# A decay-attention and soft-MoE kernel on one core: late weight loads, an early slot turn, and a second layer by column halves

## The chip, the core and the metric

The kernel runs on one core of one Trainium2 chip, as one launch. The metric is the device time in microseconds. Before the change the median of three runs is 163.58 us (163.57 to 164.32). Everything below was read from one profiled execution of that kernel, whose own time is 163.59 us.

## The reference

The work is two layers. The first is causal attention with a decay per head, done in blocks; its output, laid out as 3072 tokens of 512, is the input of a soft mixture of 8 experts with 4 slots each.

```python
# q, k, v: (4, 8, 768, 64); lam: (8,); per block of 64 tokens:
intra = einsum('bhic,bhjc->bhij', qb, kb) * Dmask        # lam ** (i - j), i >= j
out   = einsum('bhij,bhjd->bhid', intra, vb) + einsum('bhid,bhde->bhie', qb * lam_pow, state)
state = lam ** 64 * state + einsum('bhsd,bhse->bhde', kb * rev_pow, vb)

# x: (3072, 512), phi: (512, 32), w1: (8, 512, 1024), w2: (8, 1024, 512)
logits = x @ phi
d = softmax(logits, axis=0);  slot_input = (d.T @ x).reshape(8, 4, 512)
for e in range(8):
    slot_out[e] = relu(slot_input[e] @ w1[e]) @ w2[e]
out = softmax(logits, axis=1) @ slot_out
```

All data are float32. w1 and w2 are 16.8 MB each, q, k and v 6.3 MB each, and the output is 6.3 MB.

## The kernel before

**Attention.** The kernel takes chunks of 128 tokens for all heads, two sequences at a time, which it calls a pair; there are 12 pairs (NP), with p counting them. A pass over pair p runs `carried(p)` (the state's share, which reads q), `values(p)` (reads v), a copy of the result to XT by ScalarE, and `state(p)` (the state's update, which reads v and the turned keys kd). Then it starts the next pair with `scores(p + 1)`, whose products land in the PSUM banks w0 to w3 and are multiplied by the mask into `at` by four VectorE instructions, while GpSimd scales q. `turn_k` turns the keys of pair p + 1 where a state still has to be made; the last chunk of a sequence (pairs 5 and 11) needs none. Beside that, every second pass turns the exponentials e of the token softmax on TensorE (`turn_e`) and multiplies them with the tokens into slot sums (`slots`), in bank w2, from which `at` must have been read first.

**Loads.** All transfers are issued by one queue, SyncE's (SP), strictly in the order in which the code asks for them. Two homes each for q, k and v are filled two pairs ahead. w1 (32 loads of 512 KB, "early") goes into 27 slab homes and 8 others, w2 (32 loads of 512 KB, "late") into whatever is free at the end: 3 spare slabs, the homes of q, k, v, kd, mask, at, xt and x, and slabs whose w1 has been used. From p = 10 on, `next_load` puts a late load where it would have loaded q, k or v, and holds it behind a TensorE instruction of that pass (`behind`).

**The mixture.** `first(Q, ...)` multiplies the slot inputs with w1 for experts 4Q to 4Q + 3, and the result, after ReLU, is turned into hz[Q] by two VectorE instructions. The second layer multiplies hz with w2 in quads: four matmuls, one per expert, each 32 rows of the array, into four partition groups of one bank. `blocks` says in which order. FS = (4, 0) says that the first four blocks of Q = 0 come whole, 512 columns wide, and that all others are stored by column halves of 256. `second(0)` computes everything whole and the first column half's rest into bank r, and `second(1)` the rest of the second half into bank w0. The slot outputs are copied to `so`, spread over the partitions (`spread`, giving s4), and `put` makes one output tile: two matmuls, a copy by ScalarE or VectorE in turn, a transfer of 256 KB to y. There are 24 puts, 12 for each column half. PUTS and LAST say where they stand: 9 of the first half within `second(1)`, the other 15 behind it. The pair t = 0 is computed in full float32 from CR and so, with four matmul records where the others have two.

The helper class `InOrder` records all operations, so every row of the profile names line L49; the tiles tell them apart.

Of the kernel before, what the change touches and what calls it, by code (L numbers as in the profile page):

```python
# [11 lines left out]
ALU = mybir.AluOpType  # L12
# [4 lines left out]
NB = S // P  # L17
T = B * NB
HP = H // 2
D = H * DH  # L20
SL = 32
# [4 lines left out]
NP = T // 2  # L26
NSLAB = 27
NWARM = 9
FS = (4, 0)
HD = D // 2  # L30
SPARE = 3

PUTS = ((2, (0,)), (6, (9,)))
LAST = (2, 0, 1)

SENT = ((1, 1, 1, 1), (1, 1, 1, 1), (1, 0, 1, 1))
# [18 lines left out]
def decay_attn_soft_moe(  # L55
# [13 lines left out]
    pe, dve, act, pool, sp = (InOrder(tc, x) for x in (nc.tensor, nc.vector, nc.scalar, nc.gpsimd, nc.sync))  # L69
# [3 lines left out]
    loads = ctx.enter_context(tc.tile_pool(name="loads", bufs=2))  # L73
    work = ctx.enter_context(tc.tile_pool(name="work", bufs=1))
# [5 lines left out]
    def bank(tag):  # L80
        return ps.tile([P, 512], F32, tag=tag, name=tag)


    PAIR = [(b, n) for b in range(0, B, 2) for n in range(NB)]
# [19 lines left out]

    wt = {}
    early = [(Q, kc, q) for Q in range(2) for kc in range(4) for q in range(4)]
    blocks = [[], []]
    for Q in range(2):
        mid = (8 + FS[Q]) // 2
        blocks[0] += [(Q, f) for f in range(mid)]  # L110
        blocks[1] += [(Q, f) for f in range(mid, 8)]
    late = [(Q, f, i) for part in blocks for Q, f in part for i in range(2)]
    early.reverse()
    late.reverse()
# [12 lines left out]
    def load_late(pool_=None, tag="slab", bufs=None):  # L127
        Q, f, i = late.pop()
        kw = {} if bufs is None else {"bufs": bufs}
        t_ = (pool_ or slabs).tile([P, 2, 512], F32, tag=tag, name="w2t", **kw)  # L130
        go = sp.dma_start(out=t_, in_=w2[4 * Q + 2 * i:4 * Q + 2 * i + 2, f].rearrange("e p d -> p e d"))
        for y in range(2):
            wt["w2", Q, 2 * i + y, f] = t_[:, y, :]
        return go
# [9 lines left out]
    for a in range(2):  # L144
        for hh in range(2):
            sp.dma_start(
                out=phi_sb[64 * a:64 * a + 64, 2 * hh:2 * hh + 2],
                in_=phi[64 * hh:64 * hh + 64].rearrange("c (g a) s -> a c g s", a=2)[a],
# [17 lines left out]
    mask = work.tile([P, 2, HP, P], F32, tag="mask", name="mask")  # L166
    for hh in range(2):
        for hp in range(HP):
            y = hh * HP + hp
            dve.tensor_tensor_scan(  # L170
                out=mask[:, hh, hp, :],
# [34 lines left out]
    wb = [bank("w0"), bank("w1"), bank("w2"), bank("w3")]  # L206
# [6 lines left out]
    def behind(ins, earlier):  # L213
        how = mybir.DependencyInfo(mybir.DependencyClass.Sync, mybir.DependencyReason.DATA)
        tc.add_manual_dep(ins.ins, earlier.ins.name, how, reason="kept behind")
        return ins
# [27 lines left out]
    def turn_k(p, x, tk):  # L244
        for hp in range(HP):
            c = slice(hp * P, hp * P + P)
            pe.transpose(tk[:, c], IN["k", p][:, x, c], ident)
        dve.tensor_tensor(
            out=kd[:, x],
            in0=tk.rearrange("p (a b c) -> p a b c", a=HP, b=2),  # L250
            in1=kpow.broadcast_to([P, HP, 2, DH]),
            op=ALU.mult,
        )
# [17 lines left out]
    def carried(p):  # L271
        qs = IN["q", p].rearrange("p x (a i) -> p x a i", a=HP)
        first = None
        for x in range(2):
            for hp in range(HP):
                for hh in range(2):
                    mm = pe.matmul(
                        out=place(x, hh, hp),
                        lhsT=st[rows(hh), x, hp],
                        rhs=qs[rows(hh), x, hp],  # L280
                        start=(x == 0 and hp < 2),
                        stop=True,
                        skip_group_check=True,
                    )
                    first = first or mm
        return first
# [90 lines left out]
    def turn_e():  # L377
        dp = rb[:, P:2 * P]
        pe.transpose(dp, e, ident)
        act.copy(out=d, in_=dp)  # L380
# [24 lines left out]
    def next_load(p, which, at_):  # L405

        if p + 2 < NP:
            behind(load_in(p + 2, which), at_)
        else:
            behind(load_late(loads, which, 2), at_)  # L410

    def next_weights(p, point, at_):
        for _ in range(SENT[p % 3][point]):
            if early:
                behind(load_early(1), at_)
            elif run["spare"] < SPARE:
                run["spare"] += 1
                behind(load_late(bufs=NSLAB), at_)
# [7 lines left out]
    for p in range(NP):  # L426
        b, n = PAIR[p]
        even = p % 2 == 0
        more = p + 1 < NP
        g = (p - 2) // 2 if p >= 2 else None  # L430


        m1 = carried(p) if n > 0 else None
        if g is not None and even:
            new = highest(g)
            weigh(g, new)


        m2 = values(p)
        next_load(p, "k", m1 or m2)  # L440
        if p == NP - 1:
            load_late(work, "mask")
        next_weights(p, 0, m2)
        XT[p] = keep.tile([P, 2, HP, P], F32, tag="xt", name="xt", bufs=2)
        for hh in range(2):
            copy = act.copy if more or hh == 0 else dve.tensor_copy
            copy(
                out=XT[p][:, :, 2 * hh:2 * hh + 2],
                in_=xb[hh].rearrange("p (x a i) -> p x a i", x=2, a=2),
            )  # L450
        if g is not None and not even:
            gather(g)
        if n < NB - 1:
            m2 = state(p)
        next_load(p, "q", m2)
        next_weights(p, 1, m2)
        if p == NP - 2:
            load_late(work, "kd")
        if not more:
            break  # L460


        m3, m4 = scores(p + 1)
        if PAIR[p + 1][1] > 0:
            scale_q(p + 1)
        next_load(p, "v", m3)
        next_weights(p, 2, m4)


        turns = [lambda x=x: turn_k(p + 1, x, wb[x]) for x in range(2)] if PAIR[p + 1][1] < NB - 1 else []  # L470
        if g is not None and even:
            turn_e()
        m5 = m4
        if even:
            for f in turns:
                f()
        else:
            for x in range(2):
                m5 = turn_x(p - 1, x)
                for f in turns[x:x + 1]:  # L480
                    f()
            for x in range(2):
                turn_x(p, x)
        next_weights(p, 3, m5)


        if not even:
            logits((p - 1) // 2)
        elif g is not None:
            slots(g)  # L490
        if p == 0:
            reduce_selectors()
# [10 lines left out]
    g = G - 1  # L503
# [30 lines left out]
    for n, (w_, x_) in enumerate(terms):  # L534
        for kc in range(4):
            pe.matmul(
                out=si[SL * kc:SL * kc + SL, 0:P],
                lhsT=w_,
                rhs=x_.rearrange("p (h g a c) -> p g a h c", h=2, g=2, a=2)[:, kc // 2, kc % 2],
                start=(n == 0),  # L540
                stop=True,
# [118 lines left out]
    stack(three)  # L660
    assert not late

    po = bank("r")

    def quad(dst, Q, f, w, start, stop):
        for q in range(4):
            pe.matmul(
                out=dst[SL * q:SL * q + SL],
                lhsT=hz[Q][:, 4 * f + q],
                rhs=w(q),  # L670
                start=start,
                stop=stop,
                skip_group_check=True,
            )

    def second(part, dst, fill):
        todo = []
        for Q, x in blocks[part]:
            if x < FS[Q]:
                todo.append((dst, Q, x, lambda q, Q=Q, x=x: wt["w2", Q, q, x]))  # L680
            else:
                half = (8 - FS[Q]) // 2
                for i in range(2):
                    f = FS[Q] + 2 * ((x - FS[Q]) % half) + i
                    todo.append((
                        dst[:, 0:HD], Q, f,
                        lambda q, Q=Q, x=x, i=i: wt["w2", Q, q, x][:, i * HD:(i + 1) * HD],
                    ))
        for n, (d_, Q, f, w) in enumerate(todo):
            if n in fill:  # L690
                fill[n]()
            quad(d_, Q, f, w, n == 0, n == len(todo) - 1)

    so = work.tile([P, D], F32, tag="qpow", name="so")
    po1 = bank("w0")
    obanks = ("a0", "a1", "s", "w1", "w3", "r")
    nput = [0]
    s4 = []
# [27 lines left out]
        sp.dma_start(out=dst.rearrange("(a p) c -> p a c", p=P), in_=o)  # L726
        nput[0] += 1

    pairs = [(t, half) for half in range(2) for t in range(0, T, 2)]
    pairs.reverse()  # L730

    def give(n):
# [1 line left out]
            t, half = pairs.pop()  # L734
            put(t, half)

    second(0, po, {})
    act.copy(out=so[:, 0:HD], in_=po[:, 0:HD])
    dve.tensor_copy(out=so[:, HD:D], in_=po[:, HD:D])

    def split():
        s4.append(spread(len(s4)))
# [1 line left out]
    fill = {}  # L744
    for n, x in PUTS:
        fill[n] = lambda x=x: [split() if y == 0 else give(y) for y in x]
    second(1, po1, fill)
    dve.tensor_tensor(out=so[:, HD:D], in0=so[:, HD:D], in1=po1[:, 0:HD], op=ALU.add)
    for y in LAST:
        split() if y == 0 else give(y)  # L750
    give(len(pairs))
# [57 lines left out]
```

## Time and profile before

| What | Value |
|---|---|
| median of three runs | 163.58 us (163.57 to 164.32) |
| the profiled execution | 163.59 us |
| its span | 161.8 us |
| TensorE busy (matmul records) | 144.8 us, 89%, 2304 records |
| TensorE weight loads | 112.6 us, 2304 records |
| VectorE, ScalarE, GpSimd busy | 92.9, 50.9, 35.6 us |
| HBM read, written | 52.50 MB, 6.29 MB |

The profiled execution is 1.79 us longer than its span, which runs from the program's first instruction to its last. Matmul times of single records overlap, so a stretch is better read from when its records start. A float32 matmul leaves two records. The DMA share in a row by stretches is over 1 where all 16 engines work all the time: about 1.05 with loads, 1.09 with stores.

### The profile page before, as it was taken

The numbers are of one execution on the slowest core, as the hardware profiler recorded it, in microseconds if no ns is written. First come the engines' busy times: TensorE is split into PE (matmuls) and PEld (weight loads), VectorE is DVE, ScalarE is ACT, GpSimd is POOL, SyncE is SP. The second block draws the span as 40 slices with busy tenths as digits, with TensorE's granted clock in tenths as the row PEclk, the third lists the DMA queues.
The fourth block names the chain that finished last, engine by engine and source line by source line (L and its number), as shares of the span: only waits on it lengthen the run. The fifth ranks groups of instructions, "written<-read, shape, count | busy, mean of one in ns | idle before, by whom it ended". The sixth has DMA issues, their size and how long they took to land.

```text
span 161.8 us, 5407 instructions
## 1 busy us (share of the span) xinstructions
PE 144.8 (89%) x2304; PEld 112.6 (70%) x2304; DVE 92.9 (57%) x203; ACT 50.9 (31%) x118; POOL 35.6 (22%) x52
## 2 busy tenths in 40 slices
PE   6999899999997999999999899798999999999000
PEld 6988898979894989699878889476332355768000
DVE  4599581767638273938193854455589971458300
ACT  3020234202540254025402162033237951328100
POOL 1006060423206000505060511400038810000000
PEclk9999999999999999999999999999999999999855
DMA  4999999999999999999999957899999999499993
GB/s 113 358 388 410 412 413 408 409 414 409 411 418 408 412 408 415 409 413 412 409 417 397 402 222 225 300 272 359 402 407 408 402 407 406 189 313 352 383 383 127
DMA packets 30408, 59.14 MB, mean 366 GB/s; under 512 B 2736, under 2 KB 8880, under 8 KB 30384
## 3 DMA queue, kind: packets, MB, share of 16 engines
q1 hardware_dynamic: 30384, 58.80, 96.0%
q8 instruction: 18, 0.29, 0.7%
q14 instruction: 6, 0.05, 0.1%
HBM read 52.50 MB, written 6.29 MB: 363 GB/s over the span
## 4 chain that ended last, share of the span: by engine, by line
PE 68%; DMA 15%; DVE 5%; SPq 2%; issue 2%; DVEq 0%; ACT 0%; ACTq 0%
PE a L49 28%; PE w L49 25%; DMA q<-qT 10%; PE r L49 10%; DMA v<-vN 5%; PE s L49 4%; SPq L49 2%; DVE at L49 2%; DVE o L49 2%; DVE st L49 1%; DVEq L805 0%; ACT s L49 0%; DVE e L49 0%; ACTq L49 0%; DVEq L49 0%
## 5 line engine op out<-in xcount | busy, mean ns | idle before, releaser
L49 POOL TENSOR_TENSOR q<-q,qpow 128x512 f32<-128x512 f32 x20 | 25.1, 1278 | 74.9 <-PE w L49 74.9
L49 DVE TENSOR_TENSOR at<-w,mask 128x512 f32<-128x512 f32 x48 | 29.8, 684 | 6.9 <-PE w L49 6.9
L49 PE MATMUL w<-q,k 64*128 64x128 f32 x384 | 25.2, 280 | 1.1 <-DMA q<-qT 1.1
L49 PEld LDWEIGHTS w<-q,k 64*128 64x128 f32 x384 | 22.8, 189 | 2.4 <-issue 1.0
L49 ACT COPY xt<-a 128x512 f32<-128x512 f32 x23 | 12.4, 589 | 36.3 <-PE a L49 36.3
L49 PE MATMUL a<-at,v 128*64 128x128 f32 x384 | 23.6, 276 | 0.0
L49 PEld LDWEIGHTS a<-at,v 128*64 128x64 f32 x384 | 20.7, 137 | 2.1 <-issue 2.1
L49 DVE SCALAR_TENSOR_TENSOR st<-st,qpow,s 128x128 f32<-128x128 f32 x32 | 9.0, 345 | 20.2 <-PE s L49 20.2
L49 ACT COPY x<-a 128x512 f32<-128x512 f32 x22 | 12.3, 588 | 17.8 <-PE a L49 17.8
L49 PE MATMUL a<-ident,xt 128*128 128x128 f32 x96 | 13.8, 278 | 0.0
L49 PEld LDWEIGHTS a<-q,st 64*64 64x64 f32 x320 | 8.6, 132 | 5.5 <-POOL q L49 4.5
L49 DVE TENSOR_TENSOR kd<-w,mask 128x512 f32<-128x512 f32 x18 | 11.6, 683 | 0.0
L49 PE MATMUL a<-q,st 64*64 64x128 f32 x320 | 11.3, 276 | 0.1
L49 PEld LDWEIGHTS a<-ident,xt 128*128 128x128 f32 x96 | 10.6, 140 | 1.1 <-issue 0.2
L49 PE MATMUL s<-v,kd 128*64 128x64 f32 x320 | 11.1, 222 | 0.0
L49 PEld LDWEIGHTS s<-v,kd 128*64 128x64 f32 x320 | 10.6, 138 | 0.2 <-DVE kd L49 0.2
L49 PE MATMUL w<-ident,k 128*128 128x128 f32 x72 | 10.3, 274 | 0.0
L49 PE MATMUL r<-w2t,hz 128*32 128x256 f32 (+1 forms) x128 | 8.8, 432 | 0.0
L49 PEld LDWEIGHTS w<-ident,k 128*128 128x128 f32 x72 | 8.2, 141 | 0.3
L49 PE MATMUL w<-x,e 128*32 128x512 f32 (+1 forms) x72 | 6.4, 456 | 1.9 <-DVE at L49 1.8
L49 PE MATMUL a<-w1t,e 128*32 128x512 f32 x64 | 7.1, 594 | 0.5 <-DVE e L49 0.5
L49 ACT CAST ct<-part 32x256 fp32r<-32x256 f32 x18 | 7.2, 402 | 1.1 <-DVE part L49 0.9
(112 smaller groups left out, 152.6 us busy)
## 6 DMA issues: line engine op xcount, KB each, us to landing
w1t<-w_x SPq DMA_DIRECT2D x32, 512.0 KB, 9.5
w2t<-w_x SPq DMA_DIRECT2D x32, 512.0 KB, 9.4
v<-vN SPq DMA_DIRECT2D x12, 512.0 KB, 9.1
y<-o SPq DMA_DIRECT2D x24, 256.0 KB, 4.5
k<-kT SPq DMA_DIRECT2D x11, 512.0 KB, 8.7
q<-qT SPq DMA_DIRECT2D x11, 512.0 KB, 8.5
k<-kT SPq DMA_DIRECT2D x2, 256.0 KB, 3.1
q<-qT SPq DMA_DIRECT2D x2, 256.0 KB, 3.5
```

What stands on the lines that cost most here:

```text
L49: return self._tc.keep_in_program_order(f(*args, **kwargs))
```

## The change

- FS becomes (0, 0): all of w2 is stored and multiplied by column halves. `blocks` lists the eight blocks of the first half for both Q, then the eight of the second. `second(half)` computes one half into one bank (r, then w0) and copies it to its half of `so`; the add of two parts goes.
- In PUTS the 9 puts within the second half stand after 4 quads and no longer after 6. The full-precision pair t = 0 becomes the last put of each half and no longer the first.
- Late loads of the last two passes are no longer held behind a chosen matmul: each is asked for where its home's last reader has been written, and waits for that reader alone. The order becomes k, q, v, kd, k, mask, q.
- Where no keys turn (p = 4 and p = 10), `turn_e` stands ahead of `scores(p + 1)`.

```diff
-FS = (4, 0)
+FS = (0, 0)
-PUTS = ((2, (0,)), (6, (9,)))
+PUTS = ((2, (0,)), (4, (9,)))
...
+    blocks = [[(Q, x) for Q in range(2) for x in range(4 * half, 4 * half + 4)] for half in range(2)]
...
         if p + 2 < NP:
             behind(load_in(p + 2, which), at_)
-        else:
-            behind(load_late(loads, which, 2), at_)
...
+        if p == NP - 2:
+            load_late(loads, "k", 2)
         m1 = carried(p) if n > 0 else None
+        if p >= NP - 2:
+            load_late(loads, "q", 2)
...
-        if p == NP - 1:
-            load_late(work, "mask")
...
         if p == NP - 2:
+            load_late(loads, "v", 2)
             load_late(work, "kd")
...
+        if g is not None and even and not turns:
+            turn_e()
         m3, m4 = scores(p + 1)
...
+        if p == NP - 2:
+            load_late(loads, "k", 2)
+            load_late(work, "mask")
...
-        if g is not None and even:
+        if g is not None and even and turns:
             turn_e()
...
+    po = [bank("r"), bank("w0")]
+    def second(half, fill):
+        todo = [(Q, x, i) for Q, x in blocks[half] for i in range(2)]
+        for n, (Q, x, i) in enumerate(todo):
             if n in fill:
                 fill[n]()
+            for q in range(4):
+                pe.matmul(
+                    out=po[half][SL * q:SL * q + SL, 0:HD],
+                    lhsT=hz[Q][:, 4 * (2 * (x % 4) + i) + q],
+                    rhs=wt["w2", Q, q, x][:, i * HD:(i + 1) * HD],
...
+        copy = act.copy if half == 0 else dve.tensor_copy
+        copy(out=so[:, half * HD:(half + 1) * HD], in_=po[half][:, 0:HD])
...
-    pairs = [(t, half) for half in range(2) for t in range(0, T, 2)]
+    pairs = [(t, half) for half in range(2) for t in (*range(2, T, 2), 0)]
...
-    second(1, po1, fill)
-    dve.tensor_tensor(out=so[:, HD:D], in0=so[:, HD:D], in1=po1[:, 0:HD], op=ALU.add)
+    second(1, fill)
```

TensorE's order from the second layer's start to the end of the second half. Before: (w2t are weights, r, w_1829 and the a_ and s names are banks, ct and CR the softmax weights, s_1906 the spread slot outputs, so their source)

```order
L49 MATMUL r<-w2t,hz 32x512 x16
L49 MATMUL r<-w2t,hz 32x256 x48
L49 MATMUL w_1829<-w2t,hz 32x256 x8
L49 MATMUL w_1904<-so,blk 128x256
L49 MATMUL w_1829<-w2t,hz 32x256 x16
L49 MATMUL a_1925<-so,CR 128x256 x2
L49 MATMUL a_1931<-s_1906,ct 128x256 x2
```

TensorE's order in the same place after the change:

```order
L49 MATMUL r<-w2t,hz 32x256 x64
L49 MATMUL w_1828<-w2t,hz 32x256 x8
L49 MATMUL w_1903<-so,blk 128x256
L49 MATMUL w_1828<-w2t,hz 32x256 x8
L49 MATMUL a_1916<-s_1905,ct 128x256 x2
```

The 16 wide matmuls became 32 narrow ones, 16 of them in the second half; 8 matmuls and no longer 16 stand between the spread and the first put, and CR is no longer in the first put. Behind the nine puts 48 matmuls of the second half are left, where there were 24.

TensorE's order around `scores(11)` in the pass p = 10. Before: (e are the exponentials, x the tokens, the w_ names the banks of the scores)

```order
L49 MATMUL w_147<-q,k 128x128
L49 MATMUL w_146<-q,k 128x128
L49 MATMUL w_147<-q,k 128x128
L49 MATMUL r<-ident,e 128x128
L49 MATMUL w_146<-x,e 32x512 x4
L49 MATMUL a_142<-q,st 64x128
```

TensorE's order at the start of the same scores after the change:

```order
L49 MATMUL a_143<-at,v 64x128 x4
L49 MATMUL s<-v,kd 64x64 x16
L49 MATMUL r<-ident,e 128x128
L49 MATMUL w_144<-q,k 128x128
L49 MATMUL w_145<-q,k 128x128
```

The one turn of e went ahead of the 16 matmuls of the scores; the slot sums (w_146<-x,e) stay behind them.

SP's late loads from p = 10 on, numbers kept since a lower number is asked for earlier. Before, for the homes k, q, kd, v, k, mask, q:

```order
L49 DMA w2t_1415<-w2_x 128x2x512 [waits DMAHW6_49,PE_49]
L49 DMA w2t_1440<-w2_x 128x2x512 [waits DMAHW7_49,PE_49,Pool_49]
L49 DMA w2t_1442<-w2_x 128x2x512 [waits DMAHW0_49,DVE_49,PE_49]
L49 DMA w2t_1466<-w2_x 128x2x512 [waits DMAHW1_49,PE_49]
L49 DMA w2t_1506<-w2_x 128x2x512 [waits DMAHW3_49,DMAHW2_49,PE_49]
L49 DMA w2t_1508<-w2_x 128x2x512 [waits DVE_49]
L49 DMA w2t_1514<-w2_x 128x2x512 [waits DMAHW4_49,PE_49,Pool_49]
```

SP's same seven loads after the change, for the homes k, q, v, kd, k, mask, q:

```order
L49 DMA w2t_1373<-w2_x 128x2x512 [waits DMAHW6_49,PE_49]
L49 DMA w2t_1391<-w2_x 128x2x512 [waits DMAHW7_49,PE_49,Pool_49]
L49 DMA w2t_1442<-w2_x 128x2x512 [waits DMAHW0_49,PE_49]
L49 DMA w2t_1444<-w2_x 128x2x512 [waits DMAHW1_49,DVE_49]
L49 DMA w2t_1470<-w2_x 128x2x512 [waits DMAHW3_49,DMAHW2_49,PE_49]
L49 DMA w2t_1472<-w2_x 128x2x512 [waits DVE_49]
L49 DMA w2t_1494<-w2_x 128x2x512 [waits DMAHW4_49,PE_49,Pool_49]
```

The loads keep their count and nearly their order; six of the seven are asked for earlier in the program, and the rest of the queue is as it was.

## Rows read from the trace of the kernel before

**Rows 1.** Chain of work that ended last: start us, us, what.

```profile
80.23 9.27 DMA q<-qT
100.52 1.85 DVE at L49 x3
126.92 8.61 PE r L49 x128
```

**Rows 2.** Stretches: busy us (count) of PE, PEld, DVE, ACT, POOL; granted clock; DMA.

```profile
95.00:110.00 15.00, 14.09 (x269) 11.30 (x259) 6.42 (x17) 4.41 (x14) 2.51 (x2) 1.00 0.78 247
130.00:135.00 5.00, 5.00 (x96) 2.94 (x92) 2.53 (x7) 1.52 (x4) 0.29 (x1) 1.00 1.05 407
137.50:140.00 2.50, 2.50 (x34) 1.64 (x27) 0.39 (x1) 0.01 (x1) 0.00 (x0) 1.00 0.72 277
140.00:142.50 2.50, 2.50 (x32) 2.11 (x34) 2.27 (x4) 2.50 (x5) 0.00 (x0) 1.00 0.50 179
150.00:152.50 2.50, 0.00 (x0) 0.00 (x0) 1.05 (x2) 0.12 (x1) 0.00 (x0) 1.00 1.09 382
157.50:160.00 2.50, 0.00 (x0) 0.00 (x0) 0.00 (x0) 0.00 (x0) 0.00 (x0) 0.50 0.69 243
```

**Rows 3.** Timeline of SP: start us, us of the issue, what.

```profile
95.88 0.37 SPq L49 DMA_DIRECT2D w2t<-w_x  x1
131.32 0.83 SPq L49 DMA_DIRECT2D w2t<-w_x  x1
143.30 2.13 SPq L49 DMA_DIRECT2D y<-o  x1
```

**Rows 4.** Tile y, the outputs: issue ns min/median/max, first and last start; time to landing.

```profile
L49 SPq DMA_DIRECT2D y<-o x24: 372/466/2130, 140.6 to 156.0; - x24
...
DMA to landing us min/median/max: 2.3/4.5/5.2
```

**Rows 5.** Timeline of TensorE in the second layer.

```profile
126.74 8.80 PE L49 MATMUL r<-w2t,hz 128*32 128x512 f32 x128
...
136.33 0.70 PE L49 MATMUL w<-so,blk 128*128 128x256 f32 x2
136.96 1.93 PE L49 MATMUL w<-w2t,hz 128*32 128x256 f32 x32
138.82 1.13 PE L49 MATMUL a<-so,CR 128*128 128x256 f32 x4
...
141.79 2.80 PE L49 MATMUL w<-w2t,hz 128*32 128x256 f32 x48
144.52 0.74 PE L49 MATMUL w<-s,ct 128*128 128x256 f32 x4
```

**Rows 6.** Timeline of ScalarE in the second layer.

```profile
135.66 0.37 ACT L49 COPY so<-r 128x256 f32<-128x256 f32 x1 [4.08 <-PE r L49]
```

**Rows 7.** Timeline of VectorE in the second layer.

```profile
129.81 1.30 DVE L49 STREAM_TRANSPOSE hz<-h 128x512 f32<-128x512 f32 x2
...
137.47 0.43 DVE L49 TENSOR_TENSOR s<-w,s 64x256 fp32r<-64x256 f32 x1 [0.98 <-ACT s L49]
...
144.66 0.42 DVE L49 TENSOR_TENSOR so<-so,w 128x256 f32<-128x256 f32 x1 [1.95 <-PE w L49]
145.06 0.69 DVE L49 COPY o<-w 128x512 f32<-128x512 f32 x1
...
146.77 0.69 DVE L49 COPY o<-r 128x512 f32<-128x512 f32 x1
```

**Rows 8.** DMA queues over the whole span: packets, MB, share of 16 engines.

```profile
q8 instruction: 18, 0.29, 0.7%
```

**Rows 9.** DMA queues in 143.2 to 143.4 us.

```profile
q8 instruction: 1, 0.02, 53.7%
```

**Rows 10.** DMA in 143.5 to 149 us: GB/s in 40 equal slices of 0.1375 us.

```profile
GB/s 343 350 365 365 372 343 343 372 357 357 239 15 7 7 15 15 22 67 328 365 365 387 395 373 387 372 387 395 380 372 387 387 387 380 380 380 395 380 380 365
```

**Rows 11.** Timeline of TensorE in the pass p = 10.

```profile
102.51 1.07 PE L49 MATMUL w<-x,e 128*32 128x512 f32 x8 [0.91 <-DVE at L49]
```

**Rows 12.** Timeline of VectorE in the pass p = 10.

```profile
100.47 2.49 DVE L49 TENSOR_TENSOR at<-w,mask 128x512 f32<-128x512 f32 x4
```

More of the change, by code (lines that the diff above doesn't have):

```diff
@@ L106, in decay_attn_soft_moe @@
     early = [(Q, kc, q) for Q in range(2) for kc in range(4) for q in range(4)]
[L107 to L111, printed above, removed]
+    blocks = [[(Q, x) for Q in range(2) for x in range(4 * half, 4 * half + 4)] for half in range(2)]
     late = [(Q, f, i) for part in blocks for Q, f in part for i in range(2)]
@@ L460, in decay_attn_soft_moe @@
             break
+        turns = [lambda x=x: turn_k(p + 1, x, wb[x]) for x in range(2)] if PAIR[p + 1][1] < NB - 1 else []
+        if g is not None and even and not turns:
+            turn_e()
         m3, m4 = scores(p + 1)
@@ L466, in decay_attn_soft_moe @@
         next_load(p, "v", m3)
+        if p == NP - 2:
+            load_late(loads, "k", 2)
+            load_late(work, "mask")
         next_weights(p, 2, m4)
-        turns = [lambda x=x: turn_k(p + 1, x, wb[x]) for x in range(2)] if PAIR[p + 1][1] < NB - 1 else []
-        if g is not None and even:
+        if g is not None and even and turns:
             turn_e()
@@ L661, in decay_attn_soft_moe @@
     assert not late
[L663 to L689, printed above, removed]
+    po = [bank("r"), bank("w0")]
+    def second(half, fill):
+        todo = [(Q, x, i) for Q, x in blocks[half] for i in range(2)]
+        for n, (Q, x, i) in enumerate(todo):
             if n in fill:
                 fill[n]()
-            quad(d_, Q, f, w, n == 0, n == len(todo) - 1)
+            for q in range(4):
[3 more added lines that the diff above has]
+                    rhs=wt["w2", Q, q, x][:, i * HD:(i + 1) * HD],
+                    start=(n == 0),
+                    stop=(n == len(todo) - 1),
+                    skip_group_check=True,
+                )
+        copy = act.copy if half == 0 else dve.tensor_copy
+        copy(out=so[:, half * HD:(half + 1) * HD], in_=po[half][:, 0:HD])
     so = work.tile([P, D], F32, tag="qpow", name="so")
-    po1 = bank("w0")
     obanks = ("a0", "a1", "s", "w1", "w3", "r")
@@ L735, in give @@
             put(t, half)
-    second(0, po, {})
-    act.copy(out=so[:, 0:HD], in_=po[:, 0:HD])
-    dve.tensor_copy(out=so[:, HD:D], in_=po[:, HD:D])
+    second(0, {})
     def split():
```

## The prediction, made before the changed kernel was timed

> **What bounds the kernel now.** I read the chain of waits first, from its end. Its last wait for an input is pair 10's q, which lands at 89.5 us [rows 1]; from there it is TensorE almost without a break, and the break shown, at pass p = 10, is VectorE's `at`. No load of w2 stands in it: the second layer's 128 records follow each other from 126.92 in 8.61 us. So the loads may hurry as they like; they are not what TensorE waits for. Then the stretches [rows 2]. Loads run at 407 GB/s (130 to 135 us), but in 95 to 110 us at 247, which is 5.9 us of loading lost ((1 - 247/407) x 15). A share of 0.72 of 1.05 in 137.5 to 140 puts the end of the loads at about 139.2. The stores' traffic begins at 140 + 2.5 x (1 - 0.50/1.09) = 141.35, 0.75 us behind the first store's issue at 140.6 [rows 4], and ends at 157.5 + 2.5 x 0.69/1.09 = 159.1. At 382 GB/s a store of 256 KB takes 0.686 us and 24 take 16.5, so 141.35 + 16.5 = 157.8: stores fill the tail, except for 1.3 us. The tail is bound by when stores can begin and by holes among them, not by TensorE's end.
>
> The hole: SP's sixth store issue, at 143.30, took 2.13 us where the median is 0.466 [rows 3, 4], and from 144.9 to 146.0 almost nothing moves [rows 10]. In 143.2 to 143.4 a 16 KB fetch of queue 8 runs on one engine [rows 9]; there are 18 such fetches [rows 8], and 4608 TensorE records in all are 256 for each, so I take them for TensorE's instructions. The Trainium skill (Runtime: NRT & Kernel Launch, Instruction fetch mechanics) has refills in 16 KiB blocks of 256 instructions, which agrees, and calls their cost mostly hidden; the trace does not agree in the tail, where 1.3 us go. By that rule the first rival below would cost nothing, and its chance would go to the forecast.
>
> **The turn of e.** One TensorE turn goes ahead of the scores in passes 4 and 10. It fills no hole: the slot sums start at 102.51 after 0.91 us of waiting for VectorE [rows 11], whose four `at` multiplications run back to back from 100.47 in 2.49 us [rows 12]; the third, which empties the bank, ends at about 102.35 whatever e does. The turn's place afterwards was idle time. What is new is that the scores start one turn later, and VectorE may get its first bank later by as much, 0 to 0.15 us. I take +0.1 at p = 10 and nothing at p = 4, where the wait for q at 80 to 89.5 us follows.
>
> **The late loads.** Before, the first was issued at 95.88 [rows 3], held behind `carried(10)`; now it waits only for the turn of pair 10's keys, which is in the pass before. The next ones follow their homes' last readers, and nothing else stands behind them on SP but more late loads, all inputs having been asked for. The last load was issued at 131.32 [rows 3], when the queue was full. The gain in the loads' end is between 0 and 5.9 us, likely about 4, so about 135. Its worth on TensorE is 0, since no weight is waited for. Its worth for the stores is that they find free engines: without it their traffic would begin at 139.2, by what follows 0.25 us later than with it, and that is made good in the pause between batches. So 0 for this part, at either bound.
>
> **The second layer.** Records of 256 columns start every 58 ns (136.96 to 138.82, 32 of them) and 57 ns (141.79 to 144.52, 48) [rows 5]. The first part's 128 took 8.61 us; less 96 x 58 ns that leaves 3.04 us for 32 wide ones, 95 ns each. Splitting them costs 32 x (2 x 58 - 95) ns = 0.67 us. The Trainium skill (TensorE: Matmul & The Clock Gate, Back-to-back issue gap) makes the gap nearly proportional to the columns, with 2.5 ns on top: by it splitting would cost 0.08 us and the time would be 0.6 us less than mine. The rows bear it out only in part, and I go by the rows.
>
> Step by step: the start at 126.74, +0.1 from the turn. After 64 records (3.7 us, at 130.55) TensorE needs the first half of hz[1], where before it needed it after 64 records of which 32 were wide, a microsecond later. VectorE's two turns are 129.81 to 131.11 [rows 7], the first done at about 130.5: a wait of about 0.1; were both needed it would be 0.65. 128 x 58 ns = 7.42, so the first half ends at 134.36 (before: 135.35). The copy to `so` begins 0.31 us later and takes 0.37 [rows 6], the spread follows 0.3 after it: 135.34, just behind the 16 records that hide it (0.93, to 135.29). The spread takes 0.63, 16 more records 0.93: 136.90. s4 was ready 1.57 us after the spread's start (136.33 to 137.90 [rows 5, 7]), so at 136.91: the 8 matmuls between, where 16 were, just hide it. First put at 136.97. A put of two records is in SBUF 1.23 us after its start (144.52 to 145.75 [rows 5, 7]), so the first store is issued at 138.2, 2.4 us sooner, and its traffic starts at 138.95.
>
> The nine puts took 2.97 us with the full-precision pair among them (138.82 to 141.79), 20 records; 18 are 2.2 to 2.7, I take 2.4: 139.37. Then 96 records x 57 ns = 5.47: the second half ends at 144.84, 0.3 later than before (144.52). VectorE's copy of it takes the place of the add (0.42 [rows 7]), then copies the tenth put: issue at 144.84 + 1.23 = 146.07.
>
> **The tail.** First batch: 9 x 0.686 = 6.2 us from 138.95, done at 145.1, or 146.4 with the fetch's 1.3. Where does that fetch fall? It stood behind 224 records from 126.74 on (128 + 16 + 2 + 32 + 20, and 26 of the 48); the same count is reached now at 128 + 16 + 2 + 16 + 18 + 44, at 139.37 + 44 x 57 ns = 141.9: within the first batch, and made good before the second begins. Second batch: traffic from 146.07 + 0.75 = 146.8; 15 x 0.686 = 10.3. The twelfth put waits for VectorE behind s4 (146.77 + 0.69 [rows 7], +0.3, and 0.75: 148.5, with traffic done at 148.2): 0.3. End of traffic 157.4. From there to the span's end it was 161.8 - 159.1 = 2.7, one engine still being late from the fetch; an undisturbed store needs 2.3 - 0.75 - 0.69 = 0.9 to land, and 0.6 to 1.3 lie between the last landing (156.0 + 4.5 to 5.2 [rows 4]) and 161.8, so up to 2.2. I take 2.3. Span 159.7, and with the 1.79 us that lie outside it 161.5 us (this execution, 163.59, stands at the median, 163.58). What is late next is TensorE's second half: it alone now decides when the second batch starts, and the early stores leave a pause of 0.4 to 1.7 us in front of it.
>
> **Rivals.** *A fetch in the second batch.* The program has 64 more TensorE records than before (32 matmuls, each with its weight loads), and fetches come at 256 on average, unevenly. If the 18th comes after 146, or a 19th is needed, the 1.3 us recur with nothing behind to make them good: 162.8, at most 163.3 with a full 1.8. For it: the sum leaves only some 4 us of room. Against: the count above.
>
> *The second half comes late.* If TensorE waits for all of hz[1] (0.65), for s4 (0.3) and the puts take 2.7, the second batch starts 1.3 later: 162.8 to 163.3, little left of the gain. Against: hz and s4 are waited for by separate instructions, and both come out at about zero.
>
> *No pause.* If the second half were over by 144.3, stores would run from 138.95 to 155.7 without a hole: 159.8. That needs 96 records in 4.9 us, against the 57 ns of two rows.
>
> *The clock falls (slower).* TensorE is granted 2.4 GHz (1.00) throughout; it was still so in 150 to 152.5, with no matmul left, and was at 1.2 GHz (0.50) in 157.5 to 160 [rows 2]. The hole of 0.9 us at p = 10 did not lower it [rows 2, 11]. If the new waits in the second layer lowered it, the second half's 112 records would take up to 112 x 57 ns = 6.4 us more: 167.9. From half of them on it decides, being more than the 2.1 us gained. Against: the waits are 0.1 us each by my sum.
>
> **How the numbers follow.** Forecast 161.5, with 160.6 to 162.4 as its own range (0.3 each for the turn with hz, the twelfth put and the nine puts below; tail of 2.7 and both turns of hz above): 0.66. Fetch: 0.15. Late second half: 0.08. No pause: 0.05. Clock, and anything else that ends slower: 0.06. The range is 160.4 to 163.2, which leaves out the last two and the ends of the others. A difference of 0.5%, 0.8 us, is about what a measurement of this kernel tells from none: under 162.8 is faster, over 164.4 slower. Forecast, no pause and a part of the fetch case give 0.75 for faster; what is left of fetch and late half 0.18 for the same; 0.07 slower.
>
> **What would show it.** Right: loads over by about 135 with the hole in 95 to 110 mostly gone; the first half's records over at 134.4; the first store issued at 138.2; a pause in the DMA between 145 and 147; the tenth at 146.1; stores at 382 GB/s to 157.4. Wrong: TensorE idle over 0.3 us in front of hz[1] or the first put, a weight waited for, a granted clock under 1.00 before 145, or a long store issue after 147.

## The result and the profile after

The changed kernel takes 162.13 us (median of four, 161.7 to 162.21), the kernel before 163.69 us beside it (163.57 to 164.32): a ratio of 0.9892, interval 0.986 to 0.9923. That is faster by 1.56 us; 161.5 was forecast, a gain of 2.1. Here and below the ratio is worked out from the fast executions, since a few (166 to 194 us) ran slow, and so it is not exactly the quotient of the medians beside it. The profiled execution took 162.21 us, with a span of 160.4.

TensorE's timeline after, in the second layer (start us, us, what, count of records), which answers to [rows 5]:

```profile
128.02 3.64 PE L49 MATMUL r<-w2t,hz 128*32 128x256 f32 x64
132.11 3.66 PE L49 MATMUL r<-w2t,hz 128*32 128x256 f32 x64 [0.45 <-DVE hz L49]
135.58 1.05 PE L49 MATMUL w<-w2t,hz 128*32 128x256 f32 x16
136.56 0.70 PE L49 MATMUL w<-so,blk 128*128 128x256 f32 x2
...
138.28 0.71 PE L49 MATMUL a<-s,ct 128*128 128x256 f32 x4
...
140.59 5.39 PE L49 MATMUL w<-w2t,hz 128*32 128x256 f32 x96
145.91 0.74 PE L49 MATMUL w<-s,ct 128*128 128x256 f32 x4
```

The layer starts 1.28 us later than before, waits once, for hz[1], and yet comes to its first put at 138.28 where that was 138.82. The outputs after (issue ns, first and last start; time to landing), which answer to [rows 4], and the chain of waits to [rows 1]:

```profile
L49 SPq DMA_DIRECT2D y<-o x24: 372/472/765, 139.4 to 155.9; - x24
...
DMA to landing us min/median/max: 2.4/3.3/4.8
```

```profile
81.28 9.24 DMA q<-qT
...
123.52 5.35 DMA w2t<-w_x
```

The first store is issued 1.2 us sooner and no issue takes over 0.77 us, where one took 2.13. Pair 10's q lands 1.02 us later than before. The load of w2 that the chain now names ends beside a `ct` cast of VectorE (a copy that makes the softmax weights ct), and that cast follows the one before it within 0.02 us, so nothing waited for the load. Stretches after (columns as in [rows 2]), and the DMA in 141 to 149 us, in slices of 0.2 us:

```profile
95.00:110.00 15.00, 13.83 (x277) 11.14 (x276) 6.65 (x17) 4.07 (x12) 2.51 (x2) 1.00 0.84 275
137.50:140.00 2.50, 2.49 (x30) 1.95 (x23) 1.40 (x3) 1.38 (x4) 0.00 (x0) 1.00 0.67 256
140.00:142.50 2.50, 2.50 (x42) 1.65 (x44) 1.51 (x3) 1.33 (x3) 0.00 (x0) 1.00 0.97 342
145.00:147.50 2.50, 2.50 (x29) 1.73 (x22) 1.10 (x2) 0.69 (x2) 0.00 (x0) 1.00 0.72 252
147.50:150.00 2.50, 2.40 (x18) 2.00 (x17) 2.15 (x4) 1.45 (x4) 0.00 (x0) 1.00 0.70 245
157.50:160.00 2.50, 0.00 (x0) 0.00 (x0) 0.00 (x0) 0.00 (x0) 0.00 (x0) 0.50 0.54 191
```

```profile
GB/s 389 394 374 379 394 374 384 389 369 374 374 364 374 435 353 369 364 354 374 374 359 379 389 379 384 384 389 226 113 67 51 26 20 26 26 205 394 394 307 231
...
q8 instruction: 1, 0.02, 0.7%
```

The pause is there: after 27 full slices, at 146.4, the first batch is over but for one or two engines (382/16 = 24 GB/s is one), and the second batch starts at 148.0. The one fetch of queue 8 in this stretch, at 143.63, fell in the first batch. One engine then works on alone through the whole pause, and the ninth store lands only at 148.80: the pause, and the short gap behind it (307 and 231 GB/s from 148.6 to 149.0), give that engine time to catch up. The views do not name engines, so that it is the one which fetched is inferred. In 95 to 110 us the loads' rate rose from 247 to 275 GB/s, not to 407.

So that a later start does not blur it, the table counts from the second layer's first record: 126.74 before, 126.84 in the forecast, 128.02 after.

| Counted from the layer's start | before | forecast | after |
|---|---|---|---|
| first put | 12.08 | 10.13 | 10.26 |
| first store issued | 13.86 | 11.36 | 11.38 |
| tenth store issued | 20.41 | 19.23 | 19.15 |
| end of the full traffic of the stores | 32.3 | 30.6 | 30.7 |
| end of the span | 35.08 | 32.86 | 32.41 |
| last load of w2 landed | 15.06 | about 8 | 13.29 |

From the layer's start to the end the change gains 2.67 us: 1.6 because the full traffic ends sooner, and 1.0 because less follows it (2.7 us before, 1.7 after). The later start takes back 1.28, of which 1.02 is q's landing and 0.26 is TensorE's longer way from there to the layer (37.24 to 37.50 us). 1.39 are left, as the two profiled times have it (163.59 and 162.21).

### The profile page after: what moved, and what is told of

It is laid out like the page before. It is cut to its first block, busy times and chain, and to the rows that moved or that the text cites. A ratio compares the mean times of both kernels' runs of the same rounds, so it can differ in the third digit from the quotient of the medians.

```text
span 160.4 us, 5468 instructions
## 1 busy us (share of the span) xinstructions
PE 145.0 (90%) x2336; PEld 113.3 (71%) x2336; DVE 92.9 (58%) x202; ACT 50.8 (32%) x118; POOL 35.0 (22%) x52
## 4 chain that ended last, share of the span: by engine, by line
PE 68%; DMA 19%; DVE 5%; issue 1%; ACT 0%; SPq 0%; ACTq 0%; DVEq 0%
PE a L49 28%; PE w L49 25%; DMA q<-qT 16%; PE r L49 8%; PE s L49 7%; DMA w2t<-w_x 3%; DVE at L49 2%; DVE ct L49 1%; DVE h L49 0%; DVE o L49 0%; DVE hz L49 0%; DVE warm L49 0%; DVE s L49 0%; ACT s L49 0%; DVE e L49 0%
## 5 line engine op out<-in xcount | busy, mean ns | idle before, releaser
L49 PE MATMUL r<-w2t,hz 128*32 128x256 f32 x128 | 7.3, 380 | 0.4 <-DVE hz L49 0.4
```

Source lines behind the costliest of these rows:

```text
L49: return self._tc.keep_in_program_order(f(*args, **kwargs))
```

## The experiments

Theory at the start: the whole gain is in the second layer and the puts; the late loads are worth nothing; the early turn costs a quarter of a microsecond at p = 10; the rest of the later start is chance. Rivals: the sooner loads carry part of the gain, or the early turn costs the whole microsecond.

**same_again.** The changed kernel, unaltered.

> The changed kernel once more, to have its time on the chip of the next three, and a second profile of it. In its first profile pair 10's q landed 1.0 us later than in the profile before, and the first transfers of the program were already 0.9 us later, though nothing is different there. Theory (that start is chance from execution to execution): q lands between 89.4 and 90.6 us, and the first transfers differ again. Rival (the turn of e at p = 4 delays q): q lands at 90.4 or later even where the first transfers are early. Ratio to before 0.986 to 0.993 in both.

161.48 us against 164.01 (ratio 0.9856, 0.9814 to 0.9897). Pair 10's q landed at 89.67, and the layer ran as in the profile of after: first store 11.38 after its start, end 32.35. The microsecond is not the change's. The profile of after says the same. TensorE's slot sums of p = 2 and p = 4, before and then after:

```profile
32.60 1.06 PE L49 MATMUL w<-x,e 128*32 128x512 f32 x8
50.64 1.07 PE L49 MATMUL w<-x,e 128*32 128x512 f32 x8 [0.91 <-DVE at L49]
```

```profile
33.45 1.07 PE L49 MATMUL w<-x,e 128*32 128x512 f32 x8
51.69 1.07 PE L49 MATMUL w<-x,e 128*32 128x512 f32 x8 [1.17 <-DVE at L49]
```

At p = 2, ahead of the first instruction that the change moves, after is already 0.85 us late; p = 4 adds 0.20. **same_third**, once more in the last comparison, took 162.18 against 163.72 (0.9893, 0.9853 to 0.9934), with q at 90.40 and 11.39 and 32.40.

> The changed kernel a third time, beside the next three on one chip, so that some tenths of a us can be told between them. Theory: ratio 0.983 to 0.990; slot sums 13.1 us after pair 10's first score, tenth store 19.15 and the end 32.3 to 32.4 us after the second layer's start, as in both profiles so far.

In the fourteen profiles of this case q lands between 89.46 and 90.87: in eight with the early turn between 89.46 and 90.87, in five without it between 89.50 and 90.60 (fetch_sooner, with other work at p = 4, has 90.18). A quarter of a microsecond would not be seen in such a spread. What decides it stays open; it blurs every comparison of times by tenths.

**turn_back.** The turn of e behind the scores again.

```diff
-        if g is not None and even and not turns:
-            turn_e()
...
-        if g is not None and even and turns:
+        if g is not None and even:
```

> The changed kernel with the turn of e behind the scores again in passes 4 and 10. Theory (the early turn only delays VectorE's at multiplications): the slot sums start 12.9 us after the first score of pair 10 and no longer 13.1, TensorE waits 0.9 us in front of them and no longer 1.2, the second layer starts 0.2 us sooner, and the time is 0.1 to 0.4 us less than with the turn early (ratio 0.985 to 0.991). Rival (the early turn takes ScalarE's copy out of the slot sums' wait, as its place in the code suggests): 0.1 to 0.3 us more (ratio 0.990 to 0.995).

161.16 against 164.01 (0.9832, 0.9794 to 0.987); from same_again, 161.48, its time can't be told apart, so the profiles have to. TensorE at p = 10, of after and then of turn_back:

```profile
100.31 0.33 PE L49 MATMUL r<-ident,e 128*128 128x128 f32 x1
100.57 2.06 PE L49 MATMUL w<-q,k 64*128 64x128 f32 x32
103.79 1.06 PE L49 MATMUL w<-x,e 128*32 128x512 f32 x8 [1.17 <-DVE at L49]
```

```profile
99.62 2.06 PE L49 MATMUL w<-q,k 64*128 64x128 f32 x32
101.60 0.33 PE L49 MATMUL r<-ident,e 128*128 128x128 f32 x1
102.84 1.06 PE L49 MATMUL w<-x,e 128*32 128x512 f32 x8 [0.91 <-DVE at L49]
```

From the scores' start to the slot sums it is 3.22 us in both, and the turn that stands ahead adds its 0.26. Behind the scores it lay in the wait for VectorE (which is 0.91 and not 1.17 there) and cost nothing. Five profiles with the turn behind the scores have 12.87 or 12.88 us from pair 10's first score to its slot sums, eight with it ahead 13.13 or 13.14.

**loads_back.** The late loads held and ordered as before.

```diff
+        else:
+            behind(load_late(loads, which, 2), at_)
-        if p == NP - 2:
-            load_late(loads, "k", 2)
-        if p >= NP - 2:
-            load_late(loads, "q", 2)
```

> The changed kernel with the late loads asked for as before (held behind a chosen matmul, order k, q, kd, v, k, mask, q). Theory (the second column half's end on TensorE decides, loads only have to be gone by the first stores): the loads end 1 to 2 us later against TensorE's schedule, the first stores land 0.3 to 1 us later, the tenth store is issued at the same distance from the second layer's start (19.2 us), and the time is the changed kernel's within 0.4 us (ratio 0.987 to 0.994). Rival (the gain came from the sooner loads): the gain goes, 163 us or more (ratio 0.996 and over).

161.33 against 164.01 (0.9845, 0.9802 to 0.9888), the end 32.15 after the layer's start, though the last load landed 14.35 after it and the first store took 3.96 us to land. The fetch (142.11) made one issue of 1.39 us here, and the end is no later for it. That this end is 0.2 us better than same_again's has to do with VectorE's copies (below). The sooner loads carry none of the gain.

**layer_back.** The kernel before with the sooner loads and the early turn alone: the second layer, the puts and their order as before. In part:

```diff
-FS = (0, 0)
+FS = (4, 0)
-PUTS = ((2, (0,)), (4, (9,)))
+PUTS = ((2, (0,)), (6, (9,)))
```

> The kernel before with the sooner loads and the early turn alone; second layer, puts and their order as before. Theory (all of the gain is in the second layer and its puts, the early turn costs a little): ratio 1.000 to 1.003, first store about 13.9 us behind the second layer's start, the hole in the stores back at the sixth store. Rival (the sooner loads carry the gain): ratio 0.990 to 0.995.

163.98 against 164.01 (0.9993, 0.9965 to 1.0021). Its outputs and the stretch of the hole:

```profile
L49 SPq DMA_DIRECT2D y<-o x24: 372/464/1979, 141.7 to 156.9; - x24
```

```profile
145.00:147.50 2.50, 2.50 (x27) 1.82 (x16) 1.17 (x3) 0.86 (x2) 0.00 (x0) 1.00 0.71 245
```

The long issue and the hole of [rows 3, 10] are back. All of the gain is in the second layer and the puts. No run tells apart the column halves, the place of the nine puts and the later place of the pair t = 0. The end stands 34.67 us after the layer's start, 0.4 less than before; with one profile of each this is not told from chance.

**fetch_sooner.** How much of the gain is the fetch alone? The kernel before, with 14 matmuls of one column, whose results nothing reads, ahead of the slot sums in passes 4 and 10, so that every later fetch comes 112 of TensorE's instructions sooner.

```diff
+            for _ in range(0 if turns else 14):
+                pe.matmul(out=rb[0:SL, 384:385], lhsT=ident[:, 0:SL], rhs=ident[:, 0:1], start=True, stop=True)
```

> The kernel before with 28 tiny matmuls (one column, results unused) in TensorE's two idle stretches ahead of the slot sums of passes 4 and 10. They move every later 16 KB fetch of queue 8 by 112 TensorE instructions, the last one from 143.3 to about 138 us, ahead of the stores. Theory (that fetch, on one DMA engine, makes the hole in the stores): no store issue over 1 us, no hole near 145, and the time falls by 0.9 to 1.4 us (ratio 0.991 to 0.995). Rival (the hole is the queue's own, at the sixth store of a burst behind loads): the long issue and the hole stay, ratio 0.998 to 1.003.

163.16 against 163.63 (0.9965, 0.9935 to 0.9994). Stretches, and the added work at p = 10:

```profile
140.00:142.50 2.50, 2.50 (x19) 2.40 (x19) 1.16 (x2) 1.40 (x3) 0.00 (x0) 1.00 0.16 59
...
145.00:147.50 2.50, 2.50 (x27) 1.83 (x16) 1.18 (x3) 0.86 (x2) 0.00 (x0) 1.00 1.09 382
```

```profile
102.75 1.01 PE L49 MATMUL r<-ident 128*32 128x1 f32 x27 [0.35 <-ACT e L49]
```

The fetch came at 140.14, ahead of the first store (141.71); no issue took over 0.68 us, and 145 to 147.5 is full, where the DMA share was 0.69 before. The first store stands where it did (13.86 after the layer's start), the end at 33.47 and no longer 35.08. Against layer_back, whose fetch met the stores too, it is 1.2 us. So in this second layer one fetch of 16 KB costs 1.2 to 1.6 us, about half of the 2.67 that the change gains from the layer's start on. Its DMA from 156 to 162 us, in slices of 0.15 us:

```profile
GB/s 389 375 376 389 389 375 383 382 403 362 403 362 403 362 403 369 396 369 396 389 185 27 20 27 20 27 0 0 0 0 0 0 0 0 0 0 0 0 0 0
```

The full traffic ends at 159.1, 31.2 after the layer's start (before: 32.3). Even here one engine is then late by about 0.8 us. A fetch of 8 KB by another queue, 14, falls among the stores in every run (149.77 here); whether it makes this rest is not shown.

The time gained 0.5 us (0.1 to 1.1 by the interval), where 0.9 to 1.4 was expected. The added matmuls cost 0.29 us at p = 10. At p = 4 they cost 0.56 (18.60 us and no longer 18.04 from the slot sums of p = 2 to those of p = 4), and q landed 0.68 us later than in the profile of before; whether these two belong together is not shown.

**puts_at_8.** With the nine puts later in the second half the pause goes; is the first store's time then worth anything?

```diff
-PUTS = ((2, (0,)), (4, (9,)))
+PUTS = ((2, (0,)), (8, (9,)))
```

> The changed kernel with the nine puts behind 8 quads of the second half and no longer 4: the first store is issued 1.86 us later against the second layer's start (13.2 in place of 11.4 us), and the second half's end does not move. Theory (the second batch's start decides, the first batch has a pause behind it): of the 1.86 us all but the pause of 1.75 us is hidden, the tenth store is issued at 19.0 to 19.2, and the time is 0 to 0.5 us more (ratio 0.985 to 0.990). Rival (the first store's issue decides): 1.5 to 1.9 us more, ratio 0.994 to 0.998.

163.34 against 163.63 (0.9988, 0.9966 to 1.0011): nearly the whole gain is gone. My theory fell here; the time came out as the rival had it or a little above (0.994 to 0.998), but not by the rival's mechanism. The first store is issued at 13.05 and the tenth at 19.09, as early as after, and the full traffic ends 30.7 after the layer's start, as after; but the end is 33.66, 1.25 later. The DMA in the last 6 us of span in slices of 0.15 us, of puts_at_8 (157 to 163) and of after (155 to 161):

```profile
GB/s 355 396 389 389 362 396 382 389 375 389 376 389 375 362 82 48 48 48 55 21 20 27 27 20 0 0 0 0 0 0 0 0 0 0 0 0 0 0 0 0
```

```profile
GB/s 382 382 383 389 375 389 376 389 375 396 376 383 375 396 375 389 369 396 389 382 369 403 375 396 301 41 21 0 0 0 0 0 0 0 0 0 0 0 0 0
```

The fetch, at 143.99, met the sixth store (issue 1.33 us). Hardly a hole follows, but engines are behind: at 159.1, when the others are done, two of them and then one need 1.5 us more. After needs 0.4. Fetch_sooner, without a pause and with queue 8's fetch ahead of the stores, needs about 0.8. So of the 1.1 us between puts_at_8 and after, some 0.7 go with the fetch and 0.4 with the missing pause alone (an estimate from single profiles). The pause between the batches is thus no loss: in it the engines that are behind catch up.

**stack_behind.** TensorE's only wait in the layer is for hz[1], which VectorE makes behind two stacks of `ct` casts. One of them goes behind it.

```diff
-    for _ in range(2):
-        stack(three)
+    stack(three)
...
-    stack(three)
+    for _ in range(2):
+        stack(three)
```

> The changed kernel with one of the two stacks of ct copies that stand ahead of hz[1] moved behind it, so that VectorE reaches h and hz of Q = 1 some 2 us sooner. Theory (TensorE's wait for hz[1], 0.6 us of delay in the middle of the first half, is on the path): record 65 of the second layer follows without a wait, the second half and the tenth store come 0.5 to 0.65 us sooner (18.5 to 18.6 us from the layer's start), the time falls as much (ratio 0.980 to 0.984). Rival (the pause in the stores takes it up): the same time as the changed kernel, 0.985 to 0.988.

160.95 against 163.63 (0.985, 0.9818 to 0.9881). TensorE:

```profile
127.98 7.09 PE L49 MATMUL r<-w2t,hz 128*32 128x256 f32 x128
134.89 1.05 PE L49 MATMUL w<-w2t,hz 128*32 128x256 f32 x16
```

No wait is left; first store at 10.72 (11.38), tenth at 18.50 (19.15), end at 31.74 (32.4). The sixth store's issue took 1.93 us, as the fetch (142.04) met it, and the end is no later for it. **stack_second**, the same kernel in the last comparison: 161.8 against 163.72 (0.9871, 0.9826 to 0.9915), 10.72 and 31.80. So the profiles show the wait on the path, worth 0.6 to 0.7 us. The times do not show it: 0.985 lies in the rival's range, and beside same_third stack_second is 0.38 us less with intervals that overlap.

> The kernel with one stack of ct copies behind hz[1] again, against the changed kernel on the same chip. Theory (TensorE's wait for hz[1] is on the path): 0.3 to 0.7 us less than the changed kernel beside it; tenth store 18.5, end 31.7 us after the layer's start. Rival (the stores' queue takes it up): within 0.2 us of it.

**stack_turn** and **stack_turn_second**: that, and the turn back.

> As the run with the stack behind hz[1], and with the turn of e behind the scores again in passes 4 and 10. Theory: another 0.25 us less, all of it ahead of the second layer's start (slot sums 12.9 us after pair 10's first score): ratio 0.978 to 0.983. Rival (the two take up each other): no less than the stack alone.

> Stack behind hz[1] and turn of e behind the scores, again, on the same chip. Theory: 0.5 to 1.0 us less than the changed kernel beside it. Rival (its first time, no lower than the stack alone, was no chance): the same as the stack alone or more.

161.16 against 163.63 (0.9859, 0.983 to 0.9888) and 161.58 against 163.72 (0.9845, 0.9797 to 0.9893). The profiles have both gains (12.87 to 12.88 at p = 10; 10.72, and 31.8 to the end), but the times don't tell the second: it was more than stack_behind's in the one comparison and 0.2 less than stack_second's in the other.

**layer_stack.** What is of use put together: the second layer and the puts of after, the stack moved, the loads and the turn as before.

> Only the part that carried the gain, and the stack: second layer and puts of the changed kernel, one stack behind hz[1], late loads and the turn of e as in the kernel before. Theory (loads and turn give nothing, the second layer all): as the run with stack and turn, within 0.4 us, and 0.4 us or more under the changed kernel; its loads end 1 to 2 us later against the layer's start (14.0 to 15.1 us) and may meet the first stores. Rival (with stores this soon the sooner loads do matter): 0.5 us or more over the run with stack and turn.

160.83 against 163.72 (0.9831, 0.9774 to 0.9888), same_third beside it 162.18. It is the fastest of all, surely faster than before; against the changed kernel the intervals overlap. Its profile has the first store at 10.72, the end at 31.90, and one store issue of 1.83 us, as the fetch at 140.93 met the seventh store, with the pause to make it good.

## Why the prediction was right, and where it was off

**The second layer: right in sum, by two errors that cancel.** The step "Splitting costs 0.67 us" failed. In stack_behind 128 narrow records take 134.89 - 127.98 = 6.91 us, 54 ns each. The 58 and 57 ns of [rows 5] hold about 0.14 us for the change to another kind of matmul, which I spread over 32 and 48 records: 128 x 54 ns without it, and 96 x 54 ns + 0.14 = 5.32 with it, as after has (140.59 to 145.91; forecast 5.47). By that the 32 wide ones took 8.61 - 96 x 0.054 = 3.43 us, 107 ns each and not 95, and splitting costs nothing. This is what the Trainium skill had (TensorE: Matmul & The Clock Gate, Back-to-back issue gap, a gap nearly proportional to the columns, in its formula for a matmul by itself; the sustained figures of that section grow less than the columns, and these rows do not bear them out). I went by rows that I had read with the edge in them. Against that stands the wait for hz[1], 0.1 forecast and 0.63 measured (132.11 - 128.02 - 64 x 0.054): 0.25 because the faster records reach hz[1] sooner, the rest because VectorE came later. TensorE stood idle for 0.45 us in front of hz[1], which is the prediction's own sign of being wrong (over 0.3); that the sum came out all the same is luck. The first half's records end at 7.56 after the start (forecast 7.52).

VectorE after, which answers to [rows 7]:

```profile
123.88 1.32 DVE L49 COPY CR<-part 32x64 f32<-32x64 f32 x4
...
130.68 0.75 DVE L49 TENSOR_SCALAR h<-w,rown 128x512 f32<-128x512 f32 x1
131.35 1.29 DVE L49 STREAM_TRANSPOSE hz<-h 128x512 f32<-128x512 f32 x2
...
146.04 0.42 DVE L49 COPY so<-w 128x256 f32<-128x256 f32 x1 [4.54 <-PE w L49]
```

The turns of h start 3.33 us after the layer's start; before it was 3.07. The four small copies ahead of them took 1.32 us, 0.94 before. Both times occur in one and the same kernel, stack_behind and then stack_second:

```profile
123.84 0.94 DVE L49 COPY CR<-part 32x64 f32<-32x64 f32 x4
```

```profile
123.36 1.32 DVE L49 COPY CR<-part 32x64 f32<-32x64 f32 x4
```

So the late 0.25 us need not be the change's. GpSimd copies out of the same tile at that time, and its third `ct` cast goes the other way: 1.03 us where the copies are short, 0.40 where they are long. The Trainium skill (SBUF — State Buffer, SBUF: two separate sides) has a pair of ports that a GpSimd instruction and a VectorE instruction of certain kinds (in a two-port mode, or with two inputs in SBUF) hold in turn, whoever starts first, for a whole instruction. The trace agrees in that one's loss is the other's gain; no run takes GpSimd's part away, so it is not shown.

**First store, nine puts, tenth store: right** (11.36 to 11.38; 2.4 to 2.31; 19.23 to 19.15), so the first put, right behind the spread and its 16 records, and TensorE's second half as what decides the second batch.

**The fetch: right in place; the tail behind it was mis-sized.** It fell within the first batch, as counted, and no long issue came in the profile of after (0.97 us at most in same_again and same_third). "The 1.3 us" was the hole alone; the engine that is late at the end stood in the tail. Fetch_sooner shows 1.2 to 1.6 for both. The step "I take 2.3" for the tail was too careful: from the end of the full traffic (155 + 24.5 x 0.15 = 158.7) to the span's end it was 1.7. The 0.6 us, less 0.1 by which the traffic ended later than forecast, are the 0.45 by which the layer beats the sum. The Trainium skill (Runtime: NRT & Kernel Launch, Instruction fetch mechanics) calls the cost mostly hidden; after, it is, behind the pause; in before, layer_back and puts_at_8 it is not.

**The early turn: mechanism right, size off.** 0.25 and not 0.1; I had not counted that all four `at` go later by the whole start-to-start of the turn. That it costs nothing at p = 4, "where the wait for q" follows, is not shown. From the slot sums of p = 2 to those of p = 4 it is 18.24 us or more in the eight profiles with the early turn, and 18.06 or less in the five without it. The load of pair 10's q is itself issued behind TensorE, 29.59 us after the slot sums of p = 4 both before (80.23) and after (81.28), so the delay reaches its issue. Its way from issue to landing varies from 8.2 to 9.4 us, which hides whether the delay reaches the landing too.

**The late loads: the step "likely about 4" failed, "0 for this part" held.** The last load landed 0.5 us sooner (141.80 to 141.31), 1.8 against TensorE's schedule. The 139.2 that I had read for their end before was wrong as well: few engines were still busy then, but the last load landed at 141.80, after the first store was issued. Ten loads were issued between 94.6 and 110, against 11 before. From 94 to 110 us SP waited for 14.5 us in all after the change, 13.3 of them for TensorE: what holds the loads is that their homes come free at TensorE's pace, not the order of asking. I had read the missing 5.9 us as a delay that the holding made; most of it is still there with the holding gone.

**The rest** of the 0.7 us between the forecast of 161.5 and the profiled execution, 162.21, is the start: pair 10's q landed 1.02 us later and the early turn cost 0.16 more than forecast, against the 0.45 gained behind them. Most of that landing is chance (0.85 was there at p = 2). In same_again it was 0.17 later and the median is 161.48, so a hit that close is luck too.

None of the rivals came: no fetch of queue 8 in the second batch, no late second half (its wait for hz[1] came in full size, 0.63 of 0.65, but the records were faster), a pause of 1.6 us at the upper end of the forecast, and a granted clock of 1.00 till 155.

## What to carry to other kernels

A duration per record is read from two runs of different length, or the edge of a row goes into it: the same rows gave 58 ns with it and 54 without. Where transfers fill the end, look for what one engine among the sixteen carries besides: here a small fetch delayed all, unless a pause followed in which its engine caught up, and such a pause is then no waste. Differences of tenths are read against the start of the stage that they belong to, since what came before it moved by more than they do.

## What the runs showed of the hardware

- One fetch of 16 KB by queue 8 among stores: the longest issue was 0.77 us (after) to 2.13 us (before), and the fetch cost 1.2 to 1.6 us where nothing covered it (before and layer_back against fetch_sooner); ahead of the first store (fetch_sooner), no long issue followed.
- Loads of 512 KB moved 407 GB/s in a full queue (before, 130 to 135 us) and 275 where each was issued as its home came free (after, 95 to 110).
- VectorE's four copies of 32 x 64 took 0.94 or 1.32 us in two executions of one kernel (stack_behind and stack_second), and the turns of h behind them moved by 0.22 us there.
- The landing of pair 10's q, at 89.46 to 90.87 us, differs by more than a microsecond between executions, with no cause found; of after's 1.02 us, 0.85 was there at p = 2.
